# Sparse attention with a Fourier-mixing block: channel layers by Strassen products, attention in 32-query tiles

## The chip, the cores and the metric

The program runs on one core of a Trainium2 chip. A core has TensorE (PE, with its weight loads shown as PEld), VectorE (DVE), ScalarE (ACT), GpSimd (POOL) and SyncE (SP, which here issues nearly all DMAs). The metric is the device time of one launch in microseconds. Times, span and clock are those of the hardware profiler.

## The reference

Inputs are q, k, v of 4 batches x 8 heads x 768 positions x 64, and two weight matrices. The weights reach the core as 64-bit floats; everything is computed in fp32.

```python
B, H, S, D = q.shape                              # 4, 8, 768, 64
block, window = (32, 16); nb = S // block         # 24 blocks
k_sum = k.reshape(B, H, nb, block, D).max(axis=3)
v_sum = v.reshape(B, H, nb, block, D).mean(axis=3)
scores_l = where(|i - j| < window, scale * q @ k.T, -1e9)
scores_s = scale * q @ k_sum.T + np.log(block)
a = softmax(concatenate([scores_l, scores_s]))
x = a @ concatenate([v, v_sum])                   # to (B, 768, 512)
u = x + real(fft(fft(x, axis=1), axis=2))
un = (u - mean(u)) / np.sqrt(var(u) + 1e-06)
out = u + np.maximum(un @ w_ch1, 0.0) @ w_ch2     # 512x2048, 2048x512
```

## The kernel before, in words

The work of a batch has two halves, each written as a Python generator. `drive` advances several generators in turn, and a scheduler then fixes each engine's order. While post-processing of batch b - 1 (`gen_post`) is driven two steps at a time, attention of batch b (`gen_attention`) is driven one step at a time. Beside the attention of batch 0 runs `gen_weights`.

Attention works on one pair of heads (g = 0 to 3) at a time, and every batch has four pairs. `prepare` transposes k and q on PE (qk, L530) into kt and qt, and takes block maxima of k (mx, km). `scores` multiplies, for windows of 96 queries and each head, 128 keys (the weights, 64 rows each, the two heads in the two row halves of the PE array) with 96 queries (sc, L552), takes exp on ACT (L555) and multiplies by a band mask on DVE (L557). `sum_scores` does the block keys (ss, L564). `values` multiplies p with the values and a column of ones (av, L577), adds the block values (L584), and divides (L589, L590) into xs. `regroup` moves xs to x by DMA (L602). Block sums of v are made by a DVE reduction (vbs, L505) and brought into place by DMA.

`gen_weights` loads the weights in 32 chunks of 128x512 (raw, L647), converts each by four DVE operations (L651, L652, L655, L657), two on ACT and one on POOL (L659), and leaves w1 and w2 in SBUF for the rest of the program.

`gen_post` folds x (sd, zw, fg: DVE, L669), does the Fourier transforms as products with tables (y, L697 and L701; mx, L714 and L715), takes layernorm statistics, and then for each half of the 768 positions normalizes (un, L731), transposes (unt, L735), and does the two channel layers: 16 blocks n of 128 channels, four products each of 128x128 weights with 384 columns (hp, L743), relu by DVE (L746) or ACT (L748) in turn, then for three groups of 128 positions 16 products of 512 columns (ch, L754), an addition of x and the output DMA.

In the trace an fp32 matmul shows as two passes, so a row with x128 on PE has 64 matmuls. All calls of the helper `tt` carry line L669.

Of the kernel before, what the change touches and what calls it, by code (L numbers as in the profile page):

```python
# [16 lines left out]
P = 128  # L17
BLOCK = 32
W = 16
# [399 lines left out]
QT = 96  # L419
# [3 lines left out]
def _tables(S, DM):  # L423

    g = _general_consts(S, DM)
    off = np.arange(P)[:, None] - np.arange(QT)[None, :]
    band = ((off > 0) & (off < 2 * W)).astype(np.float32)

    nq = S // QT
    tok = QT * np.arange(nq)[None, :] - W + np.arange(P)[:, None]  # L430
    live = ((tok >= 0) & (tok < S)).astype(np.float32)
    return dict(band=band, live=live, fs=g["fs"], fd=g["fd"], ident=g["ident"])


def _main_program(ctx, tc, q, k, v, moe_w_ch1, moe_w_ch2, out):
# [10 lines left out]
    NQ = S // QT  # L446
    NR = NQ // 4
    nb = S // BLOCK
    S2 = S // 2
    F2 = S // 4  # L450
    HT = NST // 2
    D1 = D + 1
    assert (S, DM, D, H % 4) == (768, 512, 64, 0)
# [7 lines left out]
    spool = ctx.enter_context(tc.tile_pool(name="small", bufs=4))  # L461
    psum = ctx.enter_context(tc.tile_pool(name="psum", bufs=1, space=bass.MemoryType.PSUM))

    ident = cpool.tile([P, P], FP, name="ident")
    band = cpool.tile([P, QT], FP, name="band")
    live = cpool.tile([P, NQ], FP, name="live")
    fs = cpool.tile(list(C["fs"].shape), FP, name="fs")
    fd = cpool.tile(list(C["fd"].shape), FP, name="fd")
    eps = cpool.tile([P, 1], FP, name="eps")
    rebias = cpool.tile([P, 1], FP, name="rebias")  # L470
    w1 = cpool.tile([P, NDT, DF], FP, name="w1")
    w2 = cpool.tile([P, NIT, DM], FP, name="w2")
    rec = cpool.tile([QT, B * NP * NR, 8], FP, name="rec")


    kt_bufs = [cpool.tile([P, S + 2 * W], FP, name=f"kt{i}") for i in range(2)]
    km_bufs = [cpool.tile([P, 2, 32], FP, name=f"km{i}") for i in range(2)]
    vw_bufs = [cpool.tile([P, NQ, 2, D1], FP, name=f"vw{i}") for i in range(2)]
    vs_bufs = [cpool.tile([P, 2, D1], FP, name=f"vs{i}") for i in range(2)]

    def two_banks(name):
        return psum.tile([P, 2, 512], FP, tag="two", bufs=2, name=name)

    def one_bank(shape, name):
        return psum.tile(shape, FP, tag="one", bufs=4, name=name)
# [4 lines left out]
    def load(b, g):  # L490
        qn, kn = (apool.tile([P, NST, 2, D], FP, tag=n + "n", name=f"{n}n_{b}_{g}") for n in "qk")
# [7 lines left out]
    def block_sums(b, gg):  # L499

        raw = apool.tile([4 * nb, BLOCK, D], FP, tag="vb", bufs=1, name=f"vb_{b}_{gg}")
        nc.sync.dma_start(out=raw.rearrange("p f d -> p (f d)"),
                          in_=v[b, 4 * gg:4 * gg + 4].rearrange("h (n f) d -> (h n) (f d)", f=BLOCK))
        vb = spool.tile([4 * nb, D], FP, tag="vbs", bufs=2, name=f"vbs_{b}_{gg}")
        nc.vector.tensor_reduce(out=vb, in_=raw.rearrange("p f d -> p d f"), op=ALU.add, axis=AX.X)  # L505
        sums[b, gg] = vb

    def load_values(b, g):
        vw, vs = vw_bufs[g % 2], vs_bufs[g % 2]
        if g % 2 == 0:  # L510
            block_sums(b, g // 2)
        for e in range(2):
            src = v[b, 2 * g + e].rearrange("(t p) d -> p t d", p=QT)
            nc.sync.dma_start(out=vw[W:W + QT, :, e, 0:D], in_=src)
            nc.sync.dma_start(out=vw[0:W, 1:NQ, e, 0:D], in_=src[QT - W:QT, 0:NQ - 1, :])
            nc.sync.dma_start(out=vw[W + QT:P, 0:NQ - 1, e, 0:D], in_=src[0:W, 1:NQ, :])
            i = 2 * (g % 2) + e
            for c in range(2):
                r = 64 * c + 32 * e
                nc.sync.dma_start(out=vs[r:r + nb, e, 0:D], in_=sums[b, g // 2][nb * i:nb * (i + 1), :])  # L520

    def prepare(b, g):
# [3 lines left out]
        for src, dst in ((kn, kt[:, W:W + S]), (qn, qt)):  # L526
            for h in range(2):
                ps = one_bank([P, HT, P], f"qk_{b}_{g}_{h}")
# [318 lines left out]
```

## Time and profile before

| what | value |
|---|---|
| median of 3 runs | 1069.64 us (1069.62 to 1069.97) |
| profiled execution, its own time | 1071.54 us |
| its span | 1069.7 us |
| PE busy | 937.5 us (88%) |
| PEld busy | 564.8 us (53%) |
| DVE busy | 367.7 us (34%) |
| ACT busy | 154.6 us (14%) |
| POOL busy | 53.5 us (5%) |
| largest PE groups | hp L743 336.9 us, ch L754 333.6 us, av L577 63.0 us, sc L552 45.0 us |
| DMA | 59.57 MB, mean 56 GB/s |

Busy time is summed over the whole span, in which the first 200 us look unlike the rest: the page's row of the granted TensorE clock begins 8655555899999 and stays at 9, and the DMA row begins 6665577342121. A group's busy time counts overlapping passes once, while the mean of one instruction counts from its start to its own end.

### The profile page before, as it was taken

How to read it: one execution, taken by the hardware profiler on the slowest of the kernel's cores; microseconds unless marked ns; L12 is line 12 of the kernel's file. 1: busy time of each engine (PE TensorE's matmuls, PEld its weight loads, DVE VectorE, ACT ScalarE, POOL GpSimd, SP SyncE). 2: the span in 40 equal slices, each digit the busy share in tenths (PEclk: the TensorE clock that was granted, in tenths of full speed). 3: DMA queues.
4: the chain of work that ended last, by engine and by line, in shares of the span. 5: the costliest groups of instructions: out<-in, count | busy, mean ns of one | idle time of the engine just before them, and what ended most of it. 6: DMA issues, size and time to landing. Idle time of an engine off the chain costs nothing. (4 is left out here: it accounts for less than half of the span.)

```text
span 1069.7 us, 9582 instructions
## 1 busy us (share of the span) xinstructions
PE 937.5 (88%) x3858; PEld 564.8 (53%) x3858; DVE 367.7 (34%) x627; ACT 154.6 (14%) x284; POOL 53.5 (5%) x42
## 2 busy tenths in 40 slices
PE   5456320799999999999999999999999998999997
PEld 4344220676555545866555548765555465544543
DVE  3566869873115113641122105621131034101100
ACT  2333324221100001221001002211000010000000
POOL 0122434000000000000000000000000000000000
PEclk8655555899999999999999999999999999999999
DMA  6665577342121001222210003100100000000000
GB/s 123 220 164 157 129 219 220 73 94 67 28 74 50 0 10 50 66 52 48 47 48 1 0 20 75 36 11 5 35 10 0 20 11 0 1 10 20 1 10 22
DMA packets 109317, 59.57 MB, mean 56 GB/s; under 512 B 88656, under 2 KB 101072, under 8 KB 108368
## 3 DMA queue, kind: packets, MB, share of 16 engines
q1 hardware_dynamic: 108832, 58.75, 21.3%
q8 instruction: 32, 0.52, 0.2%
q14 instruction: 21, 0.17, 0.1%
q10 hardware_dynamic: 432, 0.12, 0.0%
HBM read 45.87 MB, written 6.29 MB: 49 GB/s over the span
## 5 line engine op out<-in xcount | busy, mean ns | idle before, releaser
L743 PE MATMUL hp<-unT,w 128*128 128x384 f32 x1024 | 336.9, 488 | 4.5 <-DVE unT L736 4.5
L754 PE MATMUL ch<-w,h 128*128 128x512 f32 x768 | 333.6, 593 | 0.0
L743 PEld LDWEIGHTS hp<-unT,w 128*128 128x128 f32 x1024 | 192.4, 190 | 139.4 <-DVE unT L736 5.4
L754 PEld LDWEIGHTS ch<-w,h 128*128 128x128 f32 x768 | 145.0, 190 | 177.9 <-issue 174.6
L746 DVE TENSOR_SCALAR h<-hp 128x384 f32<-128x384 f32 x64 | 35.7, 558 | 221.9 <-PE hp L743 216.3
L669 DVE TENSOR_TENSOR x<-ch,x 128x512 f32<-128x512 f32 x24 | 16.6, 692 | 240.2 <-PE ch L754 240.2
L748 ACT ACTIVATE h<-hp 128x384 f32<-128x384 f32 x64 | 31.4, 491 | 385.8 <-PE hp L743 385.8
L697 PE MATMUL y<-fs,fg 128*128 128x193 f32 x192 | 38.1, 347 | 53.2 <-DVE fg L688 53.2
L577 PE MATMUL av<-vw,p 128*96 128x65 f32 x512 | 63.0, 284 | 18.5 <-DMA vw<-in_v_dram 9.0
L577 PEld LDWEIGHTS av<-vw,p 128*96 128x96 f32 x512 | 59.5, 198 | 27.9 <-DMA vw<-in_v_dram 9.5
L697 PEld LDWEIGHTS y<-fs,fg 128*128 128x128 f32 x192 | 32.4, 197 | 57.6 <-DVE fg L688 51.8
L659 POOL TENSOR_TENSOR w<-w,cvt 128x512 f32<-128x512 f32 x32 | 52.1, 1633 | 132.7 <-DVE w L657 132.7
L530 PE MATMUL qk<-ident,kn 128*128 128x128 f32 x96 | 16.5, 320 | 39.6 <-DMA kn<-in_k_dram 39.6
L552 PEld LDWEIGHTS sc<-qt,kt 64*128 64x128 f32 x512 | 38.5, 218 | 19.5 <-issue 14.8
L557 DVE TENSOR_TENSOR p<-p,band 128x768 f32<-128x768 f32 x32 | 30.4, 955 | 50.9 <-ACT p L555 50.8
L552 PE MATMUL sc<-qt,kt 64*128 64x96 f32 x512 | 45.0, 315 | 2.7 <-ACT qt L531 1.9
L555 ACT ACTIVATE p<-sc 128x768 f32<-128x768 f32 x32 | 26.0, 811 | 125.3 <-PE sc L552 125.2
L530 PEld LDWEIGHTS qk<-ident,kn 128*128 128x128 f32 x96 | 13.7, 167 | 43.0 <-issue 29.3
L589 DVE RECIPROCAL rec<-av 96x8 f32<-96x8 f32 x32 | 6.5, 203 | 86.5 <-PE av L584 86.2
L653 ACT ACTIVATE cvt<-cvt,rebias 128x512 int32<-128x512 int32 x32 | 23.0, 719 | 80.0 <-DVE cvt L651 80.0
L505 DVE TENSOR_REDUCE vbs<-vb 96x64 f32<-96x2048 f32 x8 | 29.2, 3647 | 14.8 <-DMA vs<-vbs 10.3
L655 DVE SCALAR_TENSOR_TENSOR cvt<-raw,cvt 128x512 int32<-128x512 int32 x32 | 32.9, 1029 | 1.5 <-ACT cvt L653 1.5
(67 smaller groups left out, 540.6 us busy)
## 6 DMA issues: line engine op xcount, KB each, us to landing
raw<-in_moe_w_ch_dram SPq DMA_DIRECT2D x32, 512.0 KB
kn<-in_k_dram SPq DMA_DIRECT2D x32, 192.0 KB
qn<-in_q_dram SPq DMA_DIRECT2D x32, 192.0 KB
vb<-in_v_dram SPq DMA_DIRECT2D x8, 768.0 KB
vw<-in_v_dram SPq DMA_DIRECT2D x32, 192.0 KB
out_dram<-x SPq DMA_DIRECT2D x24, 256.0 KB
x<-xs SPq DMA_DIRECT2D x32, 96.0 KB
x<-xs SPq DMA_DIRECT2D x32, 64.0 KB
```

Source lines behind the costliest of these rows:

```text
L505: nc.vector.tensor_reduce(out=vb, in_=raw.rearrange("p f d -> p d f"), op=ALU.add, axis=AX.X)
L530: nc.tensor.transpose(ps[:, i, :], src[:, HT * h + i].rearrange("p e d -> p (e d)"), ident)
L552: nc.tensor.matmul(ps[:, e, QT * i:QT * (i + 1)], kt[rows, o:o + P], qt[rows, o:o + QT], start=True, stop=True)
L557: nc.vector.tensor_tensor(out=pv, in0=pv, in1=band[:, None, :].to_broadcast([P, 8, QT]), op=ALU.mult)
L577: nc.tensor.matmul(av[:, h, j % 2, e, :], p[:, e, i, :], vw[:, 4 * h + j, e, :], start=h not in first, stop=False, skip_group_check=True)
L655: nc.vector.scalar_tensor_tensor(out=ex, in0=high, scalar=-(1 << 31), in1=ex, op0=ALU.bitwise_and, op1=ALU.bitwise_or)
L659: nc.gpsimd.tensor_tensor(out=dst, in0=dst, in1=tmp[:, 0, :], op=ALU.mult)
L697: nc.tensor.matmul(y, fg[:, st, P * g:P * (g + 1)], fs[:, g % 2, par, st, :], start=(st == 0), stop=(st == HT - 1))
L743: nc.tensor.matmul(ps, w1[:, d, P * n:P * (n + 1)], unT[:, d, :], start=(d == 0), stop=(d == NDT - 1))
L746: nc.vector.tensor_scalar(out=hT[n], in0=ps, scalar1=0.0, scalar2=None, op0=ALU.max)
L748: nc.scalar.activation(out=hT[n], in_=ps, func=AF.Relu)
L754: nc.tensor.matmul(ps, hT[n][:, P * i:P * (i + 1)], w2[:, n, :], start=(n == 0), stop=(n == NIT - 1))
```

## The change

**Channel layers.** Both are computed by the Strassen-Winograd scheme: matrices are cut into 2 x 2 blocks, and 7 block products replace 8, with sums of blocks as operands. In layer 1 the left operands are quarters of w1 and their sums (7 slots in `w[P, 7, 2, P]`), the right ones are quarters of the transposed un and their sums (`u`, four DVE additions, `_right_sums`). For each of 8 blocks j there are 7 products of two matmuls with 384 columns (L863), summed in PSUM tiles hx, hy, hz and from there by ACT and DVE into the four quarters of h. In layer 2 the left operands are pieces of h with sums made on DVE (`_left_sums`, s), the right ones 7 slots of w2; the 16 hidden blocks are done in two chunks c of 4 x 2, and per chunk and per 128 rows i there are 7 products of 4 matmuls with 256 columns (L906, ox, oy, oz), each added to x by DVE.

**Weights.** 16 operand tiles (w1_0 to w1_7, w2_0 to w2_7) are made in batch 0. The sums in them are made on POOL, each tile is stored to DRAM (dw1, L706; dw2, L717), and batches 1 to 3 read it back (L722, L727). w1 tiles have 3 buffers, w2 tiles 4. Three tiles are made beside the attention of batch 0, the other 13 beside its post-processing.

**Attention.** Queries are taken in blocks of 32 with 64 keys each. Scores use 64x64 tiles of the PE array (head e and half h of the sequence at rows 64e, columns 64(e xor h); L610), values use 64x32 tiles (L638), block scores 64x32 tiles (L624). Results arrive in x's layout, so `regroup` is gone. Block sums of v are made on POOL (L529) and brought in place by one product with a selection matrix (vs, L595). A table `near` replaces `band`.

**Other.** The square root on ACT gives way to an integer start and four Newton steps on DVE (L818 to L826). The Fourier tables are read again for each batch.

```diff
 def scores(b, g):
+        ps = [abank([P, NB2, BLOCK], f"sc_{b}_{g}_{h}") for h in range(2)]
+        for i in range(NB2):
+            for h in range(2):
+                o = BLOCK * (NB2 * h + i)
+                for e in range(2):
+                    rows, r = slice(D * e, D * (e + 1)), 64 * (e ^ h)
+                    nc.tensor.matmul(ps[h][r:r + 64, i, :], kt[rows, o:o + 64], qt[rows, o:o + BLOCK],
+                                     start=True, stop=True)
...
 def values(b, g, p, pm, x):
+        for t in range(NST):
+            h = t // HT
+            for j in range(4):
+                for r in range(2):
+                    rows, i = slice(64 * r, 64 * (r + 1)), 4 * t + j
+                    nc.tensor.matmul(av[r][32 * j:32 * (j + 1), t, :], p[rows, h, i - NB2 * h, :], vw[rows, i, :],
+                                     start=(t == 0), stop=False, skip_group_check=True)
...
+def make_w1(j):
+        w = bpool.tile([P, 7, 2, P], FP, tag="w1", bufs=3, name=f"w1_0_{j}")
+        for hh in range(2):
...
+        _left_sums(gtt, lambda i: w[:, i])
+        nc.sync.dma_start(out=dw1[j], in_=w)
...
+def gen_channel(b):          # layer 1, for each j
+                product(X, A11, B11, True, False)
+                nc.scalar.copy(out=c11, in_=X)
+                product(Y, A12, B21, True, True)
+                tt(c11, Y, c11, ADD)
+                relu(c11)
+                yield
+                product(X, S2_, T2, False, False)
+                nc.scalar.copy(out=c12, in_=X)
+                product(Z, S1, T1, True, False)
+                nc.scalar.copy(out=c22, in_=Z)
+                yield
+                product(X, S3, T3, False, False)
+                tt(c22, X, c22, ADD)
+                relu(c22)
+                product(Z, S4, B22, False, True)
+                tt(c12, Z, c12, ADD)
+                relu(c12)
+                yield
+                product(X, A22, T4, False, True)
+                nc.scalar.activation(out=c21, in_=X, func=AF.Relu)
...                          # layer 2, for each chunk c and row group i
+                product(X, A11, B11, True, False)
+                tt(x11, X, x11, ADD)
+                product(Y, A12, B21, True, True)
+                tt(x11, Y, x11, ADD)
...
-    for b in range(B + 1):
-        gens = [(gen_attention(b), 1)] if b < B else []
-        gens.append((gen_post(b - 1), 2) if b else (gen_weights(), 1))
+    get_tables(0)
+    drive((gen_attention(0), 3), (gen_weights(0, 3), 1))
+    for b in range(B):
+        gens = [(gen_post(b), 4)]
+        if b == 0:
+            gens.append((gen_weights(3, None), 1))
+        if b + 1 < B:
+            gens.append((gen_attention(b + 1), 1))
         drive(*gens)
```

How the order on the engines moves, at three places. First PE in the channel layers. Before, in batch 0's first layer with attention of batch 1 between (hp: layer 1, ss and sc: scores, qk: transposes):

```order
L743 MATMUL hp_0_0_1_1327<-unT_0_0_1258,w1_77 128x384 x4
L743 MATMUL hp_0_0_2_1333<-unT_0_0_1258,w1_77 128x384 x4
L564 MATMUL ss_1_2_1351<-qt_1_2_1196,km0_82 64x384 x2
L743 MATMUL hp_0_0_3_1356<-unT_0_0_1258,w1_77 128x384 x4
L743 MATMUL hp_0_0_4_1362<-unT_0_0_1258,w1_77 128x384 x4
L552 MATMUL sc_1_2_1_1368<-qt_1_2_1196,kt0_80 128x96 x4
L743 MATMUL hp_0_0_5_1380<-unT_0_0_1258,w1_77 128x384 x4
```

After, layer 1 of batch 1 (hx, hy, hz are the three PSUM tiles of a block, the second number the block j):

```order
L863 MATMUL hx_1_1_3236<-u_1_2808,w1_1_1_3131 128x384 x2
L863 MATMUL hy_1_1_3237<-u_1_2808,w1_1_1_3131 128x384 x2
L863 MATMUL hx_1_1_3236<-u_1_2808,w1_1_1_3131 128x384 x2
L863 MATMUL hz_1_1_3238<-u_1_2808,w1_1_1_3131 128x384 x2
...
L863 MATMUL hx_1_1_3236<-u_1_2808,w1_1_1_3131 128x384 x2
L863 MATMUL hz_1_1_3238<-u_1_2808,w1_1_1_3131 128x384 x2
L863 MATMUL hx_1_1_3236<-u_1_2808,w1_1_1_3131 128x384 x2
```

Each block of layer 1 had one PSUM tile, filled once; now seven products go to three tiles, and hx is filled further after it has been read.

Second, SP's queue near the start. Before (raw: weight chunks, x from xs: the regrouping, kn and qn: k and q of pair 2):

```order
L640 DMA fd_74<-c_fd 128x1536
L647 DMA raw_0_196<-in_moe_w_ch1_dram 128x1024
L647 DMA raw_1_218<-in_moe_w_ch1_dram 128x1024
L647 DMA raw_2_253<-in_moe_w_ch1_dram 128x1024
L647 DMA raw_3_279<-in_moe_w_ch1_dram 128x1024
L647 DMA raw_4_304<-in_moe_w_ch1_dram 128x1024
L602 DMA x_0_176<-xs_0_0_263 96x2x128
```

After (vb: v for the block sums, vw: v for the values, dw1: the store of a finished operand tile):

```order
L548 DMA vb_0_1_1_340<-in_v_dram 96x1024
L578 DMA vw0_82<-in_v_dram 64x12x64 x4
L683 DMA raw_1_0_0_354<-in_moe_w_ch1_dram 128x4x256
L683 DMA raw_1_0_1_364<-in_moe_w_ch1_dram 128x4x256
L538 DMA kn_0_3_529<-in_k_dram 128x6x64 x2
L538 DMA qn_0_3_528<-in_q_dram 128x6x64 x2
L578 DMA vw1_83<-in_v_dram 64x12x64
L706 DMA dw1_0_86<-w1_0_0_353 128x1792
L578 DMA vw1_83<-in_v_dram 64x12x64 x3
L683 DMA raw_1_1_0_539<-in_moe_w_ch1_dram 128x4x256
```

The weight chunks of the start now come two at a time behind the loads of pair 2, and the store of the first operand tile stands between the value loads of pair 3.

Third, DVE in layer 1 of batch 0. Before (h from hp: relu; p with band: mask; the others belong to attention of batch 1 and block sums):

```order
L746 TENSOR_SCALAR h_0_0_0_1295<-hp_0_0_1_1327 128x384
L505 TENSOR_REDUCE vbs_2_1_2042<-vb_2_1_2040 96x64
L746 TENSOR_SCALAR h_0_0_0_1295<-hp_0_0_3_1356 128x384
L557 TENSOR_TENSOR p_1_2_1_1377<-p_1_2_1_1377,band_71 128x768
L746 TENSOR_SCALAR h_0_0_1_1296<-hp_0_0_5_1380 128x384
```

After (h from hx, hy, hz: sums of products; L867: relu; cvt and raw: conversion of w2 chunks):

```order
L867 TENSOR_SCALAR h_0_0_1527<-h_0_0_1527 128x384
L687 TENSOR_SCALAR cvt_2_0_0_1070<-raw_2_0_0_1068 128x512
L688 TENSOR_SCALAR cvt_2_0_0_1070<-raw_2_0_0_1068 128x512
L687 TENSOR_SCALAR cvt_2_0_1_1080<-raw_2_0_1_1078 128x512
L688 TENSOR_SCALAR cvt_2_0_1_1080<-raw_2_0_1_1078 128x512
L691 SCALAR_TENSOR_TENSOR cvt_2_0_0_1070<-raw_2_0_0_1068,cvt_2_0_0_1070 128x512
L693 SCALAR_TENSOR_TENSOR cvt_2_0_0_1070<-raw_2_0_0_1068,cvt_2_0_0_1070 128x512
L691 SCALAR_TENSOR_TENSOR cvt_2_0_1_1080<-raw_2_0_1_1078,cvt_2_0_1_1080 128x512
L693 SCALAR_TENSOR_TENSOR cvt_2_0_1_1080<-raw_2_0_1_1078,cvt_2_0_1_1080 128x512
L687 TENSOR_SCALAR cvt_2_1_0_1161<-raw_2_1_0_1159 128x512
L688 TENSOR_SCALAR cvt_2_1_0_1161<-raw_2_1_0_1159 128x512
L526 TENSOR_TENSOR h_0_0_1527<-hy_0_1_1654,h_0_0_1527 128x384
```

The conversions, all ahead of the fold before, now stand between the reads of layer 1's products.

More of the change, by code (lines that the diff above doesn't have):

```diff
@@ L558, in scores @@
+        for h in range(2):
+            nc.scalar.activation(out=p[:, h], in_=ps[h], func=AF.Exp, scale=SC)
+            tt(p[:, h], p[:, h], near[:, h], ALU.mult)
         return p
@@ new lines, in get_w1, with get_w2, gen_weights @@
+    def get_w1(b, j):
+        w = bpool.tile([P, 7, 2, P], FP, tag="w1", bufs=3, name=f"w1_{b}_{j}")
+        nc.sync.dma_start(out=w, in_=dw1[j])
+        wt[1, b, j] = w
+    def get_w2(b, j):
+        w = bpool.tile([P, 7, HD], FP, tag="w2", bufs=NC, name=f"w2_{b}_{j}")
+        nc.sync.dma_start(out=w, in_=dw2[j])
+        wt[2, b, j] = w
+    def gen_weights(first, last):
+        steps = [(f, j) for c in range(0, NJ, NC) for f in (make_w1, make_w2) for j in range(c, c + NC)]
+        for f, j in steps[first:last]:
+            f(j)
+            yield
@@ L737, in gen_post @@
[L737 to L748 removed]
+                ps = bank([P, 2, HD], f"mx_{b}_{t}")
```

481 lines of the change are left out of this document (278 added, 203 removed).

## The prediction

> **What bounds the kernel now.** I read the page's shares of busy time first, then a table of busy time by stretch, cut where each batch's Fourier products begin on PE, then PE's timeline, then the list of waits.
>
> ```profile
> core 0: us, PE busy (x) PEld busy (x) DVE busy (x) ACT busy (x) POOL busy (x), PEclk, DMA share, GB/s
> 0.00:203.50 203.50, 88.56 (x542) 70.58 (x542) 141.26 (x221) 64.98 (x109) 53.46 (x42) 0.58 0.62 164
> 203.50:418.30 214.80, 213.32 (x854) 123.84 (x854) 63.76 (x102) 23.98 (x46) 0.00 (x0) 1.00 0.21 49
> 418.30:643.50 225.20, 224.84 (x962) 134.00 (x962) 65.82 (x118) 28.21 (x55) 0.00 (x0) 1.00 0.16 38
> 643.50:872.90 229.40, 226.69 (x956) 135.47 (x954) 65.29 (x128) 26.63 (x53) 0.00 (x0) 1.00 0.09 24
> 872.90:1069.70 196.80, 184.14 (x550) 100.94 (x550) 31.51 (x60) 10.78 (x22) 0.00 (x0) 1.00 0.02 9
> ```
>
> There are two regimes. From 203.5 us on, PE is busy in nearly all of every stretch at granted clock 1.00 while DVE has 16 to 30% and the DMA engines at most 21%: there only PE work removed, or PE waits added, counts. In the first 203.5 us PE has 88.6 us of work, and DVE with 141.3 us sets the pace. What DVE does there, and who waits:
>
> ```profile
> 192.16 2.94 PE L697 MATMUL y<-fs,fg 128*128 128x193 f32 x8 [51.46 <-DVE fg L688]
> L655 DVE SCALAR_TENSOR_TENSOR cvt<-raw,cvt 128x512 int32<-128x512 int32 x32 | 32.9, 1029 | 1.5 <-ACT cvt L653 1.5
> L657 DVE SCALAR_TENSOR_TENSOR w<-raw,cvt 128x512 f32<-128x512 uint32 x32 | 26.0, 814 | 0.0
> L652 DVE TENSOR_SCALAR cvt<-raw 128x512 int32<-128x512 int32 x32 | 21.9, 684 | 0.0
> L651 DVE TENSOR_SCALAR cvt<-raw 128x512 int32<-128x512 int32 x32 | 16.1, 502 | 21.2 <-DMA raw<-in_moe_w_ch_dram 20.1 <-POOL w L659 1.2
> L659 POOL TENSOR_TENSOR w<-w,cvt 128x512 f32<-128x512 f32 x32 | 52.1, 1633 | 132.7 <-DVE w L657 132.7
> 53.50 1.51 PE L530 MATMUL qk<-ident,kn 128*128 128x128 f32 x6 [12.17 <-DMA kn<-in_k_dram]
> ```
>
> PE stands 51.5 us before batch 0's first Fourier product, for the fold that DVE reaches only after all 32 weight chunks: 1029 + 814 + 684 + 502 = 3.03 us of DVE each, 97 us together.
>
> **Channel layers.** These rows give the price of one pass (an fp32 matmul is two passes in the trace, so 128 means 64 matmuls); a row's own time includes the drain, so I divide the distance to the next row's start.
>
> ```profile
> 333.83 41.55 PE L743 MATMUL hp<-unT,w 128*128 128x384 f32 x128
> 375.21 41.36 PE L754 MATMUL ch<-w,h 128*128 128x512 f32 x96
> 416.51 0.87 PE L564 MATMUL ss<-qt,km 128*64 128x384 f32 x4
> 437.17 0.59 PE L715 MATMUL mx<-fd,ty 128*128 128x256 f32 x2
> 437.60 0.59 PE L714 MATMUL mx<-fd,ty 128*128 128x256 f32 x2
> ```
>
> 384 columns take 41.38 / 128 = 323 ns, 512 take 41.30 / 96 = 430 ns, 256 take 0.43 / 2 = 216 ns. Per batch the layers cost 256 x 323 + 192 x 430 = 82.8 + 82.6 = 165.4 us. After: layer 1 has 8 column blocks x 7 products x 2 row blocks = 112 matmuls of 384 columns, 224 x 323 = 72.4 us; layer 2 has 2 x 3 x 7 x 4 = 168 matmuls of 256 columns, 336 x 216 = 72.7 us. That is 145.1 us: 20.3 us less per batch, all on PE's path. The halved width costs nothing, as the mx row has the same time per column.
>
> **Attention.** One head pair before, with each row's length taken to the next row's start:
>
> ```profile
> 239.97 0.87 PE L564 MATMUL ss<-qt,km 128*64 128x384 f32 x4
> 240.76 1.56 PE L743 MATMUL hp<-unT,w 128*128 128x384 f32 x4
> 246.12 0.69 PE L552 MATMUL sc<-qt,kt 64*128 64x96 f32 x8
> 246.74 2.52 PE L743 MATMUL hp<-unT,w 128*128 128x384 f32 x7
> 252.00 0.82 PE L530 MATMUL qk<-ident,kn 128*128 128x128 f32 x6
> 252.66 0.60 PE L530 MATMUL qk<-ident,qn 128*128 128x128 f32 x4
> 258.48 1.49 PE L577 MATMUL av<-vw,p 128*96 128x65 f32 x16
> 259.90 0.69 PE L584 MATMUL av<-vs,psum 64*96 64x130 f32 x8
> 260.52 4.46 PE L743 MATMUL hp<-unT,w 128*128 128x384 f32 x13
> ```
>
> sc takes 0.62 / 8 = 78 ns a pass (32 passes, 2.5 us), ss 0.79, qk 12 x 110 = 1.3, av 1.42 / 16 = 89 (32 passes, 2.85), the block values 0.62 / 8 = 77 (16 passes, 1.24): 8.7 us, 35 us per batch. After, sc is 96 passes in four 64x64 tiles and av 96 passes in eight 64x32 tiles; no row shows such tiles. The lower end for one pass is 14 ns for sc and about 10 for av, if all tiles of a group overlap: a quarter of the 57 ns that half of qk's 110 (128 weight columns) gives for 64 columns, and an eighth of sc's 78. The upper end is 89, one after another as in untiled av. What the trace does show is that halves overlap: two row halves in sc (a pair of passes in 2 x 78 = 156, and 64-row weights) and two column halves in ss (4 passes of 384 columns in 0.79 us, 198 ns each, against 323 untiled). I take 14 for both, since the shown cases overlap, and keep 28 (only pairs overlap) and 89. Then sc 1.35, av 1.35, ss 0.79, qk 1.3, one selection product of two passes 0.25, block values 12 passes x 56 = 0.67, and 0.3 for changes between shapes (an estimate): 6.0 us a pair, 24 us per batch. Exp and mask cover the same elements (2 x 384 columns for 2 x 768 with gaps closed); they and the four x writes lie on ACT and DVE beside channel products. The x moves by DMA that vanish were off the path.
>
> By the Trainium skill, "TensorE: Matmul & The Clock Gate", Back-to-back issue gap, a pass never starts less than about 25 ns after the last one; by that 192 passes cost 4.8 us instead of 2.7 and the sum would be about 943; no run here shows 32-column passes.
>
> **What stays on PE**, and the end:
>
> ```profile
> 199.58 2.23 PE L697 MATMUL y<-fs,fg 128*128 128x193 f32 x12
> 201.74 1.36 PE L552 MATMUL sc<-qt,kt 64*128 64x96 f32 x20
> 891.79 1.54 PE L735 MATMUL unt<-ident,un 128*128 128x128 f32 x12 [2.96 <-DVE un L731]
> 895.32 0.91 PE L743 MATMUL hp<-unT,w 128*128 128x384 f32 x2 [1.99 <-DVE unT L736]
> 1063.42 0.69 DVE x L669
> ```
>
> y: 60 passes x 180 = 10.8; mx: 48 x 216 = 10.4; transposes of un: 24 x 0.117 (1.41 for 12, without the drain) = 2.8. Check on batch 1 before: 165.4 + 24 + 35 = 224.4 of 225.2 us, so the method closes. After, batches 1 and 2 have 145.1 + 24 + 24 = 193.1 us of PE work each. To this I add 8 us of waits (bounds 1 and 20): before has 0.4 to 2.7 idle, but the new products put DVE in the loop.
>
> ```profile
> L746 DVE TENSOR_SCALAR h<-hp 128x384 f32<-128x384 f32 x64 | 35.7, 558 | 221.9 <-PE hp L743 216.3
> L748 ACT ACTIVATE h<-hp 128x384 f32<-128x384 f32 x64 | 31.4, 491 | 385.8 <-PE hp L743 385.8
> L669 DVE TENSOR_TENSOR x<-ch,x 128x512 f32<-128x512 f32 x24 | 16.6, 692 | 240.2 <-PE ch L754 240.2
> ```
>
> Bank X is added to after it is read: its last product may start when the sum of c22 with X (about 0.56 us) is through, and one Z product of 4 x 323 = 1.3 us covers it. Queued ahead on DVE can be a relu, a mask or a value write, each about half a microsecond, so some of the 8 blocks and 6 row groups lose a little. DVE's total does not bind: per block 6 operations of 0.56 (8 x 3.4 = 27 us), per row group four 0.69 and seven of about 0.45 (6 x 5.9 = 35), right sums 4 x 1.0, about 34 for fold, y, mx and norm, 15 for attention: 115 of 200 us. The Newton steps replace a square root and add some 18 tiny operations of about 0.2 us per half, of which the first half lies under mx. Batch 3 has no attention: 169 + 9 of waits (before: the 5 us in the rows above, and the fold's) + 6.3 after the last product (1069.7 less 1063.4) = 184.4.
>
> **Weights through DRAM.** Each later batch reads 16 x 917 KB = 14.7 MB.
>
> ```profile
> q1 hardware_dynamic: 108832, 58.75, 21.3%
> ```
>
> 58.75 MB in 21.3% of 1069.7 us are 258 GB/s for all engines together, with mostly small packets: 57 us of a batch's 200. Layer 1 has three buffers, 9 us of products per block against 3.6 us to load one; the four of layer 2 are asked for a chunk ahead, 36 us early. I cost it at nothing; the cover is gone if the loads, which stand on SP's queue behind k, q and v loads that wait for buffers, are issued late. The stores in batch 0 wait on SP for POOL's sums, with a v load and the next raw chunk behind them.
>
> **The start.** Only 6 of 32 conversions now stand ahead of the fold: 26 x 3.03 = 79 us of DVE are gone from it, and with a fifth of the raw traffic k is no longer late (12 us above). 192.2 - 79 - 12 = 101; less 7 for two block sums that go to POOL (about 5.7 us each there by POOL's 1633 ns for 512 elements, an estimate) is 94, less some overlap: I take 90. POOL's sum before the first selection product delays scores (PE has sc behind it) by about 6 us, at the start and once more for pair 3. From there batch 0 is not PE's: fold, y, mx, norm, transposes and two or three pairs until the first layer-1 product, about 58 us (24 + 18 of PE and 16 of DVE steps between them), 148. In layer 1 of chunk 0 DVE has 16 conversions (16 x 3.03 = 48.5), 4 blocks of evacuation (13) and attention (7): 69 us against 36 + 12 on PE, 217. Then 36 for layer 2, 36 + 36 for chunk 1 and 7 for its last weights, converted at 3.03 + POOL's sums of 6 us per weight: 332. Bounds: 300 (PE-bound from 90 on: 90 + 193 + waits) and 380 (148, then DVE's 26 x 3.03 = 79 and POOL's 13 x 9 = 117 one after the other, then 36 of the last layer 2).
>
> **Sum.** 332 + 2 x 201.1 + 184.4 = 918.6, against a span of 1069.7. The profiled execution took 1071.5, 1.8 over its span; the runs' median 1069.6 is the span's own value, so I predict 918 for the median.
>
> **Rivals.**
> 1. Tiles do not overlap, and a pass costs the 89 ns of untiled av. 8 pairs lie wholly on PE's path (those of batches 2 and 3); of the 8 that run while DVE sets the pace I count half: 12 x 192 = 2304 passes x 75 ns = 173 us more, 1091: slower. It decides from 14 + 151 / 2304 = 80 ns a pass on. Against it speak ss and sc, whose halves overlap. 4%.
> 2. Only pairs overlap, so that a pass starts 28 ns after the last: 2304 x 14 = 32 more, 950. Speaks for it: pairs are all that a row shows; against it: nothing but that sc and ss show both directions. 22%. (By the Trainium skill's rule above it would be 943.)
> 3. Batch 0 stays bound by conversion: POOL's sums and DVE's operations hold each other up. The rows speak for it: L655 has a mean of 1029 beside L657's 814 of the same size while POOL works. At the upper bound of 380, 918 + 48 = 966; halfway 942. 18%.
> 4. Weight reads come late in batches 1 to 3 because of SP's order: one block's load not ahead costs 3.6 us, 16 times at most 58 a batch; half of the layer-1 blocks, 14 a batch, 960. 6%.
> 5. All new waits hide: 8 + 8 + 9 fewer and 310 for batch 0: 871. 8%.
> The forecast has the other 42%, with 895 to 940 as its own range. A measurement of this kernel can tell about 0.2% from no change; nothing but rival 1 near its deciding point would land there, 1%; slower 3%; faster 96%. Leaving out rival 1, 4's worst and a mix of 2 and 3 at the top, and half of 5 at the bottom, the range is 875 to 975.
>
> **What would show it.** Layer passes at 323 and 216 ns with 224 and 336 of them per batch; sc and av groups of 96 passes in about 1.35 us; the first y product near 90 us; the first layer-1 product near 148 and batch 0's end near 332; batch stretches of about 201; no PE wait on a weight DMA after batch 0. Wrong it would be if tile passes take over 40 ns, if PE waits on DVE or POOL for most of batch 0 beyond 350 us, or if the product chain idles PE by over 20 us a batch.

## The result, and the profile after

The changed kernel takes 953.5 us (median of 4 runs, 950.9 to 957.5) against 1069.6 us: ratio 0.892, 95% interval 0.889 to 0.895. The forecast was 918 (875 to 975), from a sum of 918.6 for the span; the span measured is 955.7, in the profiled execution, which with 957.5 us was the longest of the four. Of the four runs of same_tile_order below, one (1066.2 us) was in a slower state and is left out of its median. The same table by stretch, cut at the first Fourier product (104.5), the first layer-1 product (158.0), the ends of batch 0's four layer parts, and the starts of batches 1, 2 and 3 (a batch ends here where the next one's first Fourier product starts):

```profile
core 0: us, PE busy (x) PEld busy (x) DVE busy (x) ACT busy (x) POOL busy (x), PEclk, DMA share, GB/s
0.00:104.50 104.50, 45.95 (x1022) 35.70 (x1022) 32.05 (x82) 22.02 (x44) 26.63 (x33) 0.72 0.95 182
104.50:158.00 53.50, 42.57 (x373) 34.16 (x374) 45.21 (x116) 13.61 (x29) 12.47 (x11) 0.76 0.63 134
158.00:228.00 70.00, 53.56 (x453) 31.43 (x453) 59.66 (x90) 25.34 (x47) 38.38 (x37) 0.89 0.54 168
228.00:283.50 55.50, 48.73 (x390) 40.32 (x389) 36.89 (x63) 8.73 (x17) 17.58 (x16) 0.86 0.73 164
283.50:333.60 50.10, 40.20 (x113) 21.56 (x113) 42.08 (x56) 17.15 (x31) 34.20 (x33) 0.90 0.56 182
333.60:378.10 44.50, 39.22 (x169) 33.73 (x168) 31.27 (x56) 0.49 (x1) 9.49 (x7) 0.92 0.22 73
378.10:574.90 196.80, 194.76 (x1598) 145.73 (x1597) 103.41 (x253) 31.60 (x71) 5.42 (x6) 1.00 0.45 128
574.90:770.40 195.50, 193.54 (x1585) 144.10 (x1583) 101.88 (x255) 30.02 (x67) 0.00 (x0) 1.00 0.34 109
770.40:955.70 185.30, 172.50 (x694) 129.24 (x692) 78.99 (x193) 19.86 (x43) 0.00 (x0) 0.97 0.25 91
```

From 378.1 on the batches take about what was forecast: PE is full at clock 1.00 in batches 1 and 2, which take 196.8 and 195.5 us (forecast 201.1); batch 3 takes 185.3 (184.4). The whole miss lies ahead of it. Against the forecast's own steps: first Fourier product +14.5, from there to the first layer-1 product -4.5, the rest of batch 0 220.1 instead of 184, +36.1, batches 1 to 3 -4.3, -5.6, +0.9: together 37.1, which is 955.7 less 918.6.

The prices on PE, from the timeline (start, length, line, tile, passes):

```profile
276.26 1.20 PE L638 MATMUL av<-vw,p 64*32 64x65 f32 x96
277.39 0.94 PE L643 MATMUL av<-vs,psum 64*128 64x130 f32 x12
278.26 1.99 PE L906 MATMUL ox<-w,s 128*128 128x256 f32 x8
280.09 1.89 PE L906 MATMUL oz<-w,s 128*128 128x256 f32 x8
281.82 1.89 PE L906 MATMUL ox<-w,h 128*128 128x256 f32 x8
283.54 1.45 PE L863 MATMUL hx<-u,w 128*128 128x384 f32 x4
284.83 1.45 PE L863 MATMUL hy<-u,w 128*128 128x384 f32 x4
...
405.37 1.60 PE L610 MATMUL sc<-qt,kt 64*64 64x32 f32 x96
406.90 0.85 PE L624 MATMUL ss<-qt,km 64*32 64x384 f32 x8
```

By the distances of starts, layer 1 takes 1.29 / 4 = 323 ns a pass, layer 2 1.73 / 8 = 216, scores 1.53 / 96 = 16 and values 1.13 / 96 = 11.8.

The start: SP's issues, POOL, two 10 us stretches of the core (columns as above), and PE's waits.

```profile
48.15 0.79 SPq L578 DMA_DIRECT2D vw<-in_v_dram  x1
66.47 0.34 SPq L706 DMA_DIRECT2D dw<-w  x1
...
63.43 3.01 POOL L529 TENSOR_TENSOR w<-w 128x256 f32<-128x256 f32 x4
...
50.00:60.00 10.00, 6.84 (x112) 5.25 (x111) 5.20 (x12) 3.21 (x6) 1.06 (x1) 0.57 0.24 28
60.00:70.00 10.00, 6.29 (x214) 4.89 (x214) 5.46 (x13) 3.50 (x8) 4.45 (x6) 0.83 0.29 93
...
80.01 1.51 PE L590 MATMUL qk<-ident,kn 128*128 128x128 f32 x6 [12.03 <-DMA kn<-in_k_dram]
92.08 0.69 PE L595 MATMUL vs<-vbs,sel 96*128 96x64 f32 x2 [7.76 <-POOL vbs L529]
104.55 2.94 PE L786 MATMUL y<-fs,fold 128*128 128x193 f32 x8 [2.54 <-DVE fold L771]
```

SP stands from 48.9 to 66.5 us before the store of the first operand tile, whose sums POOL ends at 66.4. Behind the store wait three value loads, the next raw chunks and k of batch 1, and meanwhile the DMA engines' share is 0.24 to 0.29. PE then waits 12 us for that k. In all, PE's list of waits up to 104.5 us has 22.8 us for k, of which 6.1 are the first load, and 23.3 us in three places (7.4, 8.1 and 7.8) for the product behind POOL's block sums.

In batch 0's layers, DVE and POOL beside each other, DVE's conversion groups, PE's waits, and the stretch as a whole:

```profile
174.56 0.95 DVE L687 TENSOR_SCALAR cvt<-raw 128x512 int32<-128x512 int32 x1
217.09 1.49 DVE L688 TENSOR_SCALAR cvt<-raw 128x512 int32<-128x512 int32 x1
...
173.56 3.40 POOL L529 TENSOR_TENSOR w<-w 128x256 f32<-128x256 f32 x4
216.96 1.33 POOL L529 TENSOR_TENSOR w<-cvt 128x512 f32<-128x512 f32 x1 [1.28 <-PE av L643]
...
L688 DVE TENSOR_SCALAR cvt<-raw 128x512 int32<-128x512 int32 x32 | 33.2, 1038 | 0.0
L691 DVE SCALAR_TENSOR_TENSOR cvt<-raw,cvt 128x512 int32<-128x512 int32 x32 | 28.1, 877 | 1.6 <-ACT cvt L689 1.6
L693 DVE SCALAR_TENSOR_TENSOR cvt<-raw,cvt 128x512 f32<-128x512 uint32 x32 | 27.7, 864 | 0.3
L687 DVE TENSOR_SCALAR cvt<-raw 128x512 int32<-128x512 int32 x32 | 21.2, 663 | 14.3 <-DMA raw<-in_moe_w_ch_dram 11.0 <-POOL w L529 3.4
...
237.45 3.78 PE L906 MATMUL oz<-w,s 128*128 128x256 f32 x8 [3.60 <-DVE s L526]
308.01 2.93 PE L863 MATMUL hz<-u,w 128*128 128x384 f32 x4 [5.12 <-ACT h L878]
343.40 3.78 PE L906 MATMUL ox<-w,s 128*128 128x256 f32 x8 [5.28 <-DVE x L526]
...
158.00:378.10 220.10, 181.71 (x1121) 127.03 (x1121) 169.90 (x262) 51.71 (x95) 99.65 (x92) 0.89 0.53 151
```

PE is busy 182 of 220 us, at a mean clock of 0.89. PE waits 2.7 us or more seven times here, and in or right behind each of these waits the clock is 0.50 for 3.4 to 10.3 us (the row of 8 passes at 237.45 is 3.78 long, twice the 1.89 of the rows further up); of six waits of 0.7 to 2.2 us only one has such a stretch behind it. So a long wait is paid twice: PE is busy for 36 us at the half clock, which is 18 us more than at 1.00.

In this stretch no DVE conversion step that starts inside a POOL operation ends before it. The one at 217.09 ends at 218.58, POOL's multiplication of a converted chunk at 218.29. All 34 steps of L687 and L688 that start inside a POOL operation here end 0.28 to 0.30 us after it. Beside a multiplication they take 1.49 us, beside one of POOL's additions (the row at 173.56) 0.95, and alone 0.41; so the 1.49 us that the expectation of no_sums puts beside an addition belongs to a multiplication. The Trainium skill, "SBUF — State Buffer", Who interferes with whom, says that where the two engines share ports, the one that issues first keeps them for its whole instruction; the trace agrees (0.95 and 1.49 us for steps that also have rows of 0.41).

### The profile page after: what moved, and what is told of

Read it like the earlier page. It is cut to its first block, busy times and chain, and to the rows that moved or that the text cites. A ratio compares the mean times of both kernels' runs of the same rounds, so it can differ in the third digit from the quotient of the medians.

```text
span 955.7 us, 15270 instructions
## 1 busy us (share of the span) xinstructions
PE 831.0 (87%) x6386; PEld 616.0 (64%) x6386; DVE 531.4 (56%) x1158; ACT 168.8 (18%) x349; POOL 144.2 (15%) x142
## 4 chain that ended last, share of the span: by engine, by line
PE 71%; DVE 16%; DMA 4%; POOL 4%; issue 2%; SPq 1%; ACT 1%; DVEq 0%; POOLq 0%; ACTq 0%
PE ox L906 17%; PE hx L863 15%; PE oz L906 9%; PE hz L863 7%; PE oy L906 4%; PE hy L863 4%; PE y L786 3%; DVE cvt L688 3%; PE sc L610 2%; DMA vb<-in_v_dram 2%; POOL vb L529 2%; DVE cvt L693 2%; DMA raw<-in_moe_w_ch_dram 2%; PE av L638 2%; POOL w L529 1%
## 5 line engine op out<-in xcount | busy, mean ns | idle before, releaser
L863 PE MATMUL hx<-u,w 128*128 128x384 f32 x512 | 191.5, 505 | 17.9 <-DVE h L526 11.6
L863 PEld LDWEIGHTS hx<-u,w 128*128 128x128 f32 x512 | 97.7, 195 | 87.0 <-DVE h L526 15.1
L863 PE MATMUL hz<-u,w 128*128 128x384 f32 x256 | 95.0, 493 | 7.3 <-ACT h L878 7.3
L906 PE MATMUL ox<-w,s 128*128 128x256 f32 x384 | 95.6, 393 | 5.6 <-DVE x L526 5.6
L906 PE MATMUL oz<-w,s 128*128 128x256 f32 x384 | 95.1, 391 | 3.6 <-DVE s L526 3.6
L906 PE MATMUL ox<-w,h 128*128 128x256 f32 x384 | 90.9, 385 | 0.0
L906 PEld LDWEIGHTS ox<-w,s 128*128 128x128 f32 x384 | 74.4, 197 | 18.5 <-DVE x L526 7.7
L906 PEld LDWEIGHTS oz<-w,s 128*128 128x128 f32 x384 | 75.5, 197 | 15.3 <-DVE s L526 4.3
L906 PEld LDWEIGHTS ox<-w,h 128*128 128x128 f32 x384 | 74.4, 194 | 12.7 <-issue 0.6
L863 PEld LDWEIGHTS hz<-u,w 128*128 128x128 f32 x256 | 48.9, 192 | 43.1 <-ACT h L878 7.1
L529 POOL TENSOR_TENSOR w<-cvt 128x512 f32<-128x512 f32 x32 | 44.2, 1385 | 95.4 <-DVE cvt L693 75.3
L529 POOL TENSOR_TENSOR w<-w 128x256 f32<-128x256 f32 x64 | 55.3, 879 | 2.8
L863 PE MATMUL hy<-u,w 128*128 128x384 f32 x128 | 47.9, 495 | 0.0
L906 PE MATMUL oy<-w,h 128*128 128x256 f32 x192 | 45.7, 380 | 0.0
L867 DVE TENSOR_SCALAR h<-h 128x384 f32<-128x384 f32 x96 | 40.8, 425 | 2.9
L529 POOL TENSOR_TENSOR vb<-vb,vb 96x1024 f32<-96x1024 f32 x8 | 20.3, 2531 | 135.8 <-DMA vb<-in_v_dram 135.8
L526 DVE TENSOR_TENSOR x<-oz,x 128x256 f32<-128x256 f32 x48 | 20.3, 423 | 36.2 <-PE oz L906 36.1
```

Of the source, the lines that this page charges most:

```text
L526: nc.vector.tensor_tensor(out=out, in0=in0, in1=in1, op=op)
L529: nc.gpsimd.tensor_tensor(out=out, in0=in0, in1=in1, op=op)
L863: nc.tensor.matmul(ps, w[:, a, kk, :], u[:, r, kk, :], start=start and kk == 0, stop=stop and kk == 1, skip_group_check=True)
L867: nc.vector.tensor_scalar(out=t, in0=t, scalar1=0.0, scalar2=None, op0=ALU.max)
L906: nc.tensor.matmul(ps, left[a][:, n, :], wt[2, b, j][:, r, :], start=start and n == 0, stop=stop and n == NC - 1, skip_group_check=True)
```

## The experiments

Landmarks of every kernel's timeline, in us (rest = span less end of batch 0). They come from one profiled execution each; in the rounds of these runs the kernel before took 1069.6 to 1071.7 us, to which the ratios go.

| kernel | first Fourier product | first layer-1 product | end of batch 0 | span | rest | median | ratio to before (95%) |
|---|---|---|---|---|---|---|---|
| before | 192.2 | 232.0 | 418.4 | 1069.7 | 651.3 | 1069.6 | 1 |
| attention_alone | 185.7 | 224.8 | 396.8 | 1028.6 | 631.8 | 1029.9 | 0.962 (0.958 to 0.966) |
| changed | 104.5 | 158.0 | 378.1 | 955.7 | 577.6 | 953.5 | 0.892 (0.889 to 0.895) |
| stores_pool | 102.5 | 147.8 | 362.4 | 939.4 | 577.0 | 940.2 | 0.877 (0.875 to 0.879) |
| sums_dve | 97.3 | 148.0 | 355.2 | 935.4 | 580.2 | 935.5 | 0.873 (0.871 to 0.875) |
| no_sums | 109.9 | 156.0 | 352.0 | 929.0 | 577.0 | 932.5 | 0.871 (0.869 to 0.873) |
| no_dve_convert | 107.9 | 152.2 | 351.8 | 928.0 | 576.2 | 930.2 | 0.869 (0.867 to 0.871) |
| stores_pool_sums_dve | 103.4 | 143.8 | 358.0 | 930.2 | 572.2 | 929.7 | 0.868 (0.865 to 0.871) |
| block_sums_dve | 98.1 | 145.9 | 356.2 | 929.7 | 573.5 | 926.2 | 0.864 (0.861 to 0.868) |
| relu_act | 96.5 | 140.9 | 335.8 | 911.1 | 575.3 | 913.5 | 0.853 (0.850 to 0.857) |
| tables_later | 86.9 | 139.9 | 344.0 | 919.2 | 575.2 | 920.5 | 0.859 (0.856 to 0.862) |
| floor | 90.8 | 135.7 | 312.9 | 889.8 | 576.9 | 892.8 | 0.834 (0.830 to 0.837) |
| convert_ahead | 177.9 | 276.7 | 435.3 | 1011.4 | 576.1 | 1012.5 | 0.945 (0.943 to 0.948) |
| same_tile_order | 125.4 | 184.8 | 411.4 | 1057.7 | 646.3 | 1059.5 | 0.986 (0.976 to 0.995) |

In all kernels with the new layers and the tile order of the change the rest is 572 to 580 us; what differs is batch 0.

**stores_pool.** The theory: SP's hold. The rival: the bytes at the start.

```diff
-        nc.sync.dma_start(out=dw1[j], in_=w)
+        nc.gpsimd.dma_start(out=dw1[j], in_=w)     # dw2 alike
```

> The 16 stores of finished operand tiles to DRAM are issued from POOL's queue instead of SP's; nothing else changes. Reason 1 (queue order): in the changed kernel SP stands from 48.9 to 66.5 us before the first store, waiting for POOL's sum of that tile, with three value loads, the next raw chunks and the k load of batch 1 behind it, while the DMA engines are at 24 to 29%. If that hold sets the start, the first Fourier product comes about 12 to 17 us earlier (near 90 instead of 104.5), and the median falls from 953.5 to about 938. Reason 2 (the DMA rate bounds the start: share 0.95 of 104.5 us): the same bytes have to pass, the start moves by under 4 us and the median stays within 950 to 954.

13.3 us less, so the stores on SP cost something, but not by the way expected: the first Fourier product comes only 2 us sooner. The 12 us wait for k of batch 1 is gone, and PE waits at the next step instead, for POOL's block sums:

```profile
86.12 0.69 PE L595 MATMUL vs<-vbs,sel 96*128 96x64 f32 x2 [13.76 <-POOL vbs L529]
102.46 2.94 PE L786 MATMUL y<-fs,fold 128*128 128x193 f32 x8 [9.11 <-DVE fold L771]
```

The gain shows later: 10 us at the first layer-1 product, 16 at the end of batch 0.

**no_sums and sums_dve.** Operand sums left out, or made on DVE.

```diff
-        _left_sums(gtt, lambda i: w[:, i])                       # both tiles' sums, POOL
+        nc.scalar.copy(out=w[:, 4:7], in_=w[:, 0:3])             # no_sums
+        _left_sums(tt, lambda i: w[:, i])                        # sums_dve
```

> The sums in the weight operands (four POOL additions per tile) are left out; ACT copies fill the three slots, so the products are computed on other numbers and the layers' work is unchanged. Reason 1 (POOL's sums hold DVE up and come late: L688 has 1038 ns on DVE in the changed kernel against 684 before, and DVE instructions that start during a POOL addition last 1.49 instead of 0.42 us): 13 tiles lose 3.5 us of POOL and some 2 us of DVE delay each, batch 0 ends 25 to 30 us earlier, median about 925. Reason 2 (the four DVE operations of a conversion set the pace alone): batch 0 ends less than 8 us earlier, median 945 to 953.

> The sums in the weight operands are made on DVE instead of POOL. Cost on DVE: four additions of 128x256, about 0.35 us each, 1.4 us per tile, 18 us over the 13 tiles beside batch 0's layers. Reason 1 (POOL and DVE hold each other up): DVE gets about 2 us per tile back and the tile is ready some 2 us sooner, so the end is the same or up to 15 us earlier, median 938 to 953. Reason 2 (DVE's own operations set the pace): 13 x 1.4 = 18 us more on DVE, of which at least half shows: median 962 to 972.

No sums: batch 0 ends 26 us earlier, as expected (25 to 30) and far above the rival's 8; the median falls by 21 us, less than expected. On DVE: 18 us less although DVE has more to do, better than the range given. Its conversion rows, to be held against the four above, and the layers of batch 0 as a whole:

```profile
L688 DVE TENSOR_SCALAR cvt<-raw 128x512 int32<-128x512 int32 x32 | 26.3, 822 | 0.0
L691 DVE SCALAR_TENSOR_TENSOR cvt<-raw,cvt 128x512 int32<-128x512 int32 x32 | 24.5, 767 | 3.1 <-ACT cvt L689 3.1
L693 DVE SCALAR_TENSOR_TENSOR cvt<-raw,cvt 128x512 f32<-128x512 uint32 x32 | 22.1, 690 | 0.2
L687 DVE TENSOR_SCALAR cvt<-raw 128x512 int32<-128x512 int32 x32 | 17.0, 532 | 9.4 <-DMA raw<-in_moe_w_ch_dram 6.1 <-POOL w L529 3.3
...
148.00:355.20 207.20, 179.79 (x1221) 125.80 (x1220) 156.55 (x316) 51.19 (x97) 52.29 (x40) 0.93 0.55 160
```

With POOL's additions gone, the four means add up to 2.81 us a chunk (822 + 767 + 690 + 532) instead of 3.44, and DVE is busy 156.6 us in the layers instead of 169.9, although it does the additions itself. So POOL's additions cost more by holding DVE than the same additions cost on DVE.

**no_dve_convert.**

```diff
-        nc.vector.tensor_scalar(out=ex, in0=high, scalar1=0x7FF00000, ...)    # and three more on DVE
+        nc.scalar.activation(out=tmp[:, 0, :], in_=raw[:, :, 1], func=AF.Copy, scale=2.0 ** -31)
+        nc.scalar.activation(out=tmp[:, 1, :], in_=raw[:, :, 0], func=AF.Copy, scale=2.0 ** -31)
```

> The four DVE operations of each weight conversion are left out (ACT makes two plain copies of the integers, POOL multiplies them and makes the sums as before), so the weights are other numbers and the layers' work is unchanged. If conversion on DVE is what bounds batch 0, the time from the first layer-1 product to the end of batch 0 falls from 220 us to near PE's own work of 145 + 18 = 163 plus POOL's part, about 175 to 185, and the median to 910 to 920. If loads, queue order or POOL's sums set the pace, it stays above 200 us and the median above 935.

Measured 930: neither. The layers of batch 0 still take 199.6 us, with PE busy 172.9. DVE is busy only 87.7 us there, so something else holds the layers. PE's waits there are spread: 7.4 us for ACT's copies of products, 7.3 for DVE's sums into x, 5.1 for a tile behind POOL's sum, 4.1 for POOL's block sum. No single one of these causes has the 36 us to itself; each edit alone ends batch 0 at 352 to 362.

**stores_pool_sums_dve and block_sums_dve.** Both edits, and then v's block sums on DVE too (`gtt` to `tt` in `block_sums`).

> Both of the two edits together: stores of operand tiles issued from POOL's queue, and the operand sums made on DVE. Apart they gave 940.2 and 935.5 us against 953.5. If they remove two things (SP's hold at the start, and the mutual hold of POOL and DVE in the layers of batch 0), the gains add: about 922. If both only make the first store ready or harmless sooner (one cause, SP's hold), the gains overlap: 933 to 938.

> As the run with both edits, and the block sums of v are also made on DVE (five additions of 1024 down to 64 columns, about 2.8 us, instead of 5.3 us on POOL), so POOL has only the multiplications of the conversions and the store issues. In the changed kernel PE waits 7.4, 8.1 and 7.8 us at the start and 2.9 us in batch 0 for the selection product behind POOL's block sums. If POOL's speed and queue made that wait, 3 to 5 us go at each of three places, 8 to 14 us in all below the run with both edits. If the load of v is what comes late, it changes by under 3 us.

929.7 lies between: 24 us, three quarters of the sum of the two gains (13.3 + 18). 926.2 (923.98 to 931.9, the trace being of the longest run) is not clearly better: the first Fourier product comes 5 us sooner, and batch 0 ends where it did. PE's three waits at the start for the block sums fall from 28.2 us (7.3, 7.2, 13.7) to 22.5 (5.6, 6.2, 10.8): POOL's slower additions made a few us of them, less than the 3 to 5 at each place that were expected. What makes the rest was not separated, and that removing these waits shortens the whole is not shown.

**relu_act and tables_later.**

```diff
+                    if b == 0:
+                        nc.scalar.activation(out=t, in_=t, func=AF.Relu)          # relu_act
...
-    get_tables(0)
-    drive((gen_attention(0), 3), (gen_weights(0, 3), 1))
+    drive((gen_attention(0), 3), (gen_start(), 1))    # weights 0, 1, then tables, then weight 2
```

> As the run with stores from POOL, operand sums and block sums on DVE, and the three relus per layer-1 block of batch 0 go from DVE to ACT. DVE loses 24 x 0.4 = 10 us in batch 0's layer 1, where it is full; ACT has room there. If DVE's sum of work sets the pace: 916 to 920. If the order of conversions ahead of the product reads does, or ACT's own conversion steps come later now: 924 to 930.

> As the run with relus on ACT, and the Fourier tables (3 MB) are asked for after the loads of three head pairs instead of after two. The DMA engines are at 100 to 120% of their mean share from 0 to 80 us, and PE waits 6 to 11 us for k and v of pairs 2 to 4. If the order of bytes on the queue matters there, these come up to 10 us sooner and the first Fourier product (98 us) too: 5 to 10 us less than the run with relus on ACT. If the amount of bytes before the first Fourier product sets it, no change within 3 us.

The relus bring 12.6 us, more than their own 10, and DVE's busy time in the layers falls by as much (168.2 to 155.7). That fits DVE's work as the pace of batch 0's layers, with a higher clock (0.92 to 0.96) where PE waits less; that a product's chain has one DVE operation less would help too, and the two were not separated. Of the layers of batch 0 in block_sums_dve, relu_act and floor (one row each):

```profile
145.90:356.20 210.30, 179.32 (x1019) 123.34 (x1018) 168.22 (x329) 50.78 (x96) 43.61 (x39) 0.92 0.53 158
...
140.90:335.80 194.90, 170.90 (x1000) 118.05 (x999) 155.66 (x298) 60.93 (x115) 45.03 (x39) 0.96 0.54 164
...
135.70:312.90 177.20, 162.37 (x909) 115.90 (x908) 122.58 (x225) 48.30 (x92) 41.42 (x39) 0.97 0.58 181
```

Tables later: the first Fourier product comes 9.6 us sooner, as expected, and the whole gets 7 us longer. The order on the queue matters at the start, but by the first layer-1 product the lead is down to 1 us: PE waits 9.0 us there before a selection product until a layernorm operation on DVE is through, where relu_act has 2.6. Why the layers then take 9 us longer is not shown.

**floor.**

> Stores from POOL's queue, operand sums and block sums of v on DVE (926 us together), and besides the four DVE operations of each conversion left out (two plain ACT copies instead; the weights are other numbers). If after those three edits conversion on DVE is what still holds batch 0 (358 us to its end, DVE busy 18 to 20 of each 20 us in its layer-1 stretches), batch 0 ends near PE's own work from the first layer-1 product on: 146 + 145 + 25 = 316 and the median is 885 to 895. If PE's waits on its own product chain or the halved clock after short waits hold it, the end stays above 340 and the median above 910.

892.8, in the range: with conversion off DVE after the other edits, batch 0's layers take 177 us with PE busy 162. This is not the least possible: POOL's multiplications still hold DVE, and five relus there take 1.8 to 3.1 us instead of 0.34. Of the 61 us between the changed kernel and this bound, edits that leave nothing out brought 27 (926.2) and, with the relus, 40 (913.5).

**attention_alone.** The kernel before with the attention of the change, nothing else.

> The kernel before with only the new attention (32-query blocks, tiles, v block sums on POOL, no regrouping); channel layers, weight conversion ahead of batch 0 and the square root as before. By the forecast's steps a pair costs 2.7 us less PE time, 11 us per batch in the three batches that run beside layers, 33 us, and the start loses 8 to 29 us of DVE reductions, of which the half that lies there counts for 5 to 10: about 1028. If attention was hidden at the start and its PE time is cheap anyway, 1045 or more; the rest of the change's 116 us would then be the layers and the moved conversion.

1029.9 against 1028 expected. Its stretches (start, batch 0 to 3):

```profile
0.00:185.70 185.70, 59.86 (x1361) 46.55 (x1361) 122.00 (x209) 61.98 (x111) 67.94 (x58) 0.65 0.84 187
185.70:396.80 211.10, 210.81 (x1161) 121.39 (x1161) 53.56 (x112) 21.34 (x47) 14.98 (x14) 0.99 0.19 41
396.80:612.40 215.60, 215.31 (x1488) 125.42 (x1486) 58.67 (x122) 24.96 (x56) 5.83 (x6) 1.00 0.20 39
612.40:824.30 211.90, 209.16 (x1356) 120.23 (x1354) 54.70 (x120) 21.07 (x46) 0.00 (x0) 1.00 0.10 20
824.30:1028.60 204.30, 190.87 (x582) 106.41 (x580) 36.47 (x72) 12.12 (x26) 0.00 (x0) 0.99 0.03 10
```

The new layers (with the reading of weights from DRAM and the Newton steps, which no run takes apart from them) then bring 18.8, 16.4 and 19.0 us in batches 1, 2 and 3 (215.6 to 196.8, 211.9 to 195.5, 204.3 to 185.3), near the 20.3 of the forecast. Batch 0 ends at 378.1 instead of 396.8, 18.7 sooner, which is about the layers' gain alone: the Fourier products start 81 us sooner, and all of it is given back by the end of batch 0.

**same_tile_order.**

```diff
-        for i in range(NB2):            # scores; values alike
-            for h in range(2):
-                for e in range(2):
+        for h in range(2):
+            for e in range(2):
+                for i in range(NB2):
```

> The changed kernel with its score and value products in another loop order: all 12 (scores) or 6 (values) products of one PE tile one after the other, where the changed kernel goes through the four or eight tiles in turn. Same products and counts. If tiles overlap because neighbours use different tiles (the forecast's step: 14 ns a pass instead of 57 for a lone 64-column weight load), a pass costs 40 to 57 ns in scores and 27 to 57 in values, 96 passes of each 2.5 to 5.5 us instead of 1.5 and 1.1, so 4 to 8 us more per pair and 40 to 90 us on the 8 to 12 pairs on PE's path: 990 to 1045. If a pass has a price of its own whatever the order (the floor of rival 2), nothing changes: 950 to 957.

1059.5, beyond the range: the order in which the tiles are used is worth 106 us (116 is the gain of the whole change). The rival (a price per pass whatever the order) falls. The loop order also changes how often neighbours write different PSUM tiles (`ps[h]`), but that is not the cause: in a score group of this run passes start 58 ns apart within a tile, and near each of the three changes of tile one starts 5 to 6 ns after the last, although two of these changes stay in the same PSUM tile. Three stretches of batch 1, values, scores, and what follows on PE:

```profile
436.38:440.56 4.18, 4.18 (x98) 4.09 (x97) 1.59 (x4) 0.00 (x0) 0.00 (x0) 1.00 0.29 85
448.50:453.90 5.40, 5.40 (x97) 5.35 (x96) 3.05 (x16) 0.49 (x1) 0.00 (x0) 0.93 0.79 226
453.90:458.00 4.10, 4.10 (x23) 2.82 (x22) 2.95 (x15) 2.35 (x5) 0.00 (x0) 0.50 0.13 28
```

A pass costs 44 ns in values and 56 in scores, as expected, 6.9 us more a pair (9.58 against 2.66). The rest (646.3 against 577.6, 8.6 us for each of 8 pairs) has a second part: late in the scores and behind them the clock is 0.50 although PE never stood still. It is so at all eight score groups of batches 1 and 2 in this run, for 3.4 to 6.8 us each, and at none of the changed kernel's.

**convert_ahead.**

```diff
-    drive((gen_attention(0), 3), (gen_weights(0, 3), 1))
+    drive((gen_attention(0), 1), (gen_weights(0, None), 1))   # batch 0 reads the tiles back from DRAM too
```

> The changed kernel with all 16 operand tiles made beside the attention of batch 0, as the kernel before has its conversions, stored to DRAM, and read back for batch 0 as for the other batches. So the new layers and attention stay, and only the moving of conversions behind the fold is undone. The forecast's account: moving them is worth 45 us (first Fourier product 104 instead of about 192, batch 0 longer by some 40), so undoing it gives about 995. The other account, from attention alone (1030, 41 us) and the layers' 4 x 20 us: these make up the whole 116 us, so the early start is given back inside batch 0, and undoing it gives 945 to 960, with the first Fourier product at 185 to 195 and batch 0 after it as long as batch 1, 197 us.

1012.5: above both. The stretch between the first Fourier product and the first layer-1 product shows why it is no clean undoing:

```profile
177.90:276.70 98.80, 46.83 (x579) 36.20 (x579) 84.06 (x158) 23.17 (x46) 47.89 (x44) 0.67 0.71 215
```

Conversion is not done at 178 us but goes on for most of the next 99 us (POOL is busy 47.9 us there). The likely reason, not tested, is that with three buffers and a store in SP's queue after each tile the tiles come slower than the chunks of the kernel before. So 59 us bounds from above what the moving is worth; that it gave back what it won follows from the attention run, by subtraction, and a version with the kernel before's pace of conversion was not tried, nor one with the new layers alone.

The fastest version with all of the computation in it is relu_act: 913.5 us, ratio 0.853 to the kernel before (interval 0.850 to 0.857).

## Why the prediction was right, and where it was off

- **Channel layers** (20.3 us a batch, 323 and 216 ns): right. 16 to 19 us in batches 1 to 3 by subtraction, prices to the nanosecond, and the waits put at 8 us a batch were 2 (196.80 less 194.76).
- **Attention** (6.0 us a pair, 14 ns a pass): right; 16 and 11.8 ns, and the attention alone came within 2 us of the 1028 that these terms gave. The overlap on which the step rests was shown by taking it away. The rivals with 28 and 89 ns fall, although the median alone would have fitted the first of them (950); only the pass prices tell them apart. The 25 ns between starts that the Trainium skill ("TensorE: Matmul & The Clock Gate", Back-to-back issue gap) gives as a floor do not hold either for tiles that take turns: 11.8 and 16 measured.
- **Weights through DRAM** (nothing): right: PE waits for no weight DMA in batches 1 to 3, with the DMA share at 0.45, 0.34 and 0.25.
- **The start** (90 us): 104.5. Two steps failed. "k is no longer late": after the first load PE still waits 16.7 us for it, 12.0 of them behind the store on SP, which "wait on SP for POOL's sums" named without a price (SP stood 17.5 us). And the wait for POOL's block sums, put at about 6 us twice, was 7.4, 8.1 and 7.8. Neither is shown to be worth the 14.5 us: with the stores off SP the start came 2 us sooner, with the operand sums off POOL 7, with the tables later besides the other edits 17.6.
- **Batch 0 after that** (184 us from the first layer-1 product): 220. The mechanism was named, as rival 3 with 18% (942 to 966): POOL's sums and DVE hold each other up. Taking the sums off POOL brought 18 to 21 us, and the trace shows the holds. The mis-sized terms: layer 1 of chunk 0, the one part for which DVE's work was added up, was put at 69 us and took 70. The other three parts were put at 36 each, with 7 more for the last weights, as if no attention and hardly a conversion or sum lay beside the products; they took 55.5, 50.1 and 44.5. Two things were missing from the sum: a conversion took 3.44 us of DVE instead of 3.03 beside POOL's additions, and PE ran 36 us at the half clock behind its waits, 18 us more than at 1.00, for which the forecast had no term. The forecast's 332 us for the end of batch 0 was nearly reached only by the fourth edit (335.8).
- The chances: the forecast's own band (895 to 940) was missed; the range held because rival 3 was in it. That the total for batches 1 to 3 came within 9 us is not luck, since its passes and their prices came out; the median's place in the range says little by itself.

## What to carry to other kernels

Small products gain from PE tiles when neighbours in the queue use different tiles; the loop order decides, and a wrong one cost 106 us here, where the whole new attention had brought 40. An in-order queue that must wait for a sum to store it holds the loads behind it: price each such wait by what stands behind it. When work is moved from a stretch that it bounded into one that PE bounded, recount every engine of the new stretch, mutual holds and the clock after short waits included.

## What the runs showed of the hardware that I had not expected

- Lone-tile passes one after the other (96 of 64x64, 56 ns apart, PE busy 5.40 of 5.40 us) were followed by a granted clock of 0.50 for the next 4.1 us; the same passes in turn over four tiles left it at 1.00. So a busy PE alone does not keep the clock up. What the clock goes by stays open: it fell at all eight score groups of batches 1 and 2 in the one run with this order, but not at its value groups (96 passes of 64x32, 44 ns apart, 4.2 us).
- Moving POOL's additions to a DVE that was already busy 170 of 220 us made DVE's conversion faster (3.44 to 2.81 us a chunk) and the kernel 18 us shorter. A DVE step can be held over several POOL operations in a row: in stores_pool one of 0.41 us took 5.98 beside four of them (at 181.88). DVE sums that read a product from PSUM were not held: in the layers of batch 0 those into h took 0.54 us beside POOL and 0.55 without.
